# Retention and two MLPs on one core: padded queries, narrower states, and another order in the opening

## The chip, the cores and the metric

The kernel runs on one core of a Trainium2 chip. The metric is the device time of one execution in microseconds. Three runs of the kernel before gave 868.02, 868.12 and 868.51 us; the median is 868.12 us.

## What is computed

Four batches, 8 heads, 576 positions, head width 64. A retention (attention without softmax, with a decay by distance) is followed by two MLPs of width 512 to 2048 to 512 on 2304 tokens.

```python
scores = (1 / np.sqrt(64)) * np.matmul(q, k.transpose(0, 1, 3, 2))
gamma = 1.0 - 2.0 ** (-5.0 - np.arange(H))
ret = scores * np.where(rel >= 0, gamma[:, None, None] ** rel, 0.0)   # rel = row position - column position
x = np.matmul(ret, v).transpose(0, 2, 1, 3).reshape(2304, 512)
h = x @ moe_w_in;   x = softplus(h) @ moe_w_out
h = x @ moe2_w_in;  out = (h * sigmoid(1.702 * h)) @ moe2_w_out
```

## The kernel before

Heads are taken in pairs, two heads stacked on the 128 partitions (`halves`, L278). The positions of a batch go in chunks of 128: pair (b, p) has a first step c = 0 with chunks 0 and 1 and a second step c = 1 with chunks 2 and 3 and the last 64 positions. One batch has 8 such steps; the text numbers them 0 to 7, step i being pair i//2, c = i%2. The program is written out in full and each engine works through its own instructions in the order of the text.

One step of the retention is `step` (L301). It forms for each chunk a state update (`sums`, L336: decayed keys times values, in PSUM), the scores of the chunk (L345, into `ps`), and, for the step `out_i` handed in beside it, the output products: states times queries (L323) and masked scores times values (L326, L328). Behind them come: the states taken from PSUM (`svs`, one tile of 128x128 for two heads, whose two 64x64 blocks on the diagonal are filled one by one, L354 to L361; the rest was set to zero once at L470), the scores scaled into `a` (ACT at L366 in the first batch) and masked by GpSimd's affine_select (L370), the tail's scores (L378), and the output times its decay into `xf` (L384) and `xt` (L389).

The first batch is `first_batch` (L415): loads of all 8 steps of keys, queries and values (`kqv`, 512 KB each), the batch's last positions (`ends`, 640 KB at once), decays, and the raw words of the first weights (`w1_load`, two transfers of 512 KB each for one f), all on the SP queue. Then ten rounds follow: round i does `scale_pair(i + 1, True)` (L297, both halves of the keys times their decay, on GpSimd), `step(i - 2, i)`, in odd rounds from 3 on `split_x` (the result is split into a high part on ACT, `xh`, and a low part on DVE, `xl`, which waits in `late` for the next round), and one warming product (`warm`, L458). `warm` is also called WARM = 14 times at the start, on a tile that nothing else uses.

The weights of the first MLP arrive as 64-bit words and are converted by `convert` (L100), a generator of five pieces per weight f: ACT L109, then DVE L121 and L122, then DVE L126, then ACT L92 (the high half), then DVE L97 (the low half, which is followed by L109 of the next f). The loop at L502 advances it once per round from index 4 on, the index being the round plus one. After the rounds `pre` (L1039) loads f + 4 and advances it until f + 2 weights are made; `side` (L512) advances it and the retention of the next batch (`batch`, L396, one third of a step at a time) between the products of the first MLP. That MLP is `run_first` (L149): `mm1(f)`, 12 products with `w1_in[f]`, softplus, and two turns later `mm2(f)`, 12 products with `w1_out[f]`; all of them are recorded on L147. The tiles of the weights, the raw words and the loads of the first batch share one pool, `wp`, with 16 places.

Of the kernel before, what the change touches and what calls it, by code (L numbers as in the profile page):

```python
# [15 lines left out]
P = 128  # L16
# [5 lines left out]
WARM = 14  # L22
# [10 lines left out]
def kernel(  # L33
# [190 lines left out]
    with tc.manual_schedule():  # L224
# [37 lines left out]
        with ExitStack() as consts, ExitStack() as right, ExitStack() as second:  # L262
# [4 lines left out]
            mask = ac.tile([P, 5, D], F32, name="mask")  # L267
# [4 lines left out]
            svs = [[ac.tile([P, P], F32, name=f"sv{i}_{j}") for j in range(4)] for i in range(2)]  # L272
# [8 lines left out]
            def load_pair(i, tile_of=None, end_of=None):  # L281
# [7 lines left out]
                v = t[:, 2 * C0:].rearrange("p (t s d) -> p t s d", t=2, s=2)  # L289
                loaded[i] = t[:, 0:C0], t[:, C0:2 * C0], v[:, :, 0, :], v[:, :, 1, :], e  # L290

            def scale_pair(i, pool=False):
                p, x = pairs[i][2], loaded[i][2]
                for h in range(2):
                    y, d = x[:, :, halves[h]], sdec[:, 2 * p + h:2 * p + h + 1]
                    if pool:
                        nc.gpsimd.tensor_scalar(out=y, in0=y, scalar1=d, scalar2=None, op0=ALU.mult)  # L297
                    else:
                        nc.scalar.mul(y, y, d)

            def step(out_i, i, banks, on_act, later, early=False):  # L301
# [12 lines left out]
                if out_i is not None:  # L314
# [4 lines left out]
                    for t in range(2 + c):  # L319
                        j = slice(t * P, t * P + (P if t < 2 else D))  # L320
                        if states[t] is not None:
                            for h, r in enumerate(halves):
                                put(h, j, states[t][:, r], q[:, j] if t < 2 else e[:, P:P + D])  # L323
                        for h, r in enumerate(halves):
                            if t < 2:
                                put(h, j, v[:, t, r], a[:, h * C0 + t * P:h * C0 + (t + 1) * P])  # L326
                            else:
                                put(h, j, e[:, P + D + h * D:P + D + (h + 1) * D], a[:, 2 * C0:])  # L328
                if i is not None:
                    b, c, p = pairs[i]  # L330
                    k, q, x, v, e = loaded[i]
                    if c:
                        for h, r in enumerate(halves):
                            put(h, ends_at, e[:, r], e[:, P:P + D])
# [15 lines left out]
                if i is not None:  # L350
                    b, c, p = pairs[i]
                    states = [None] + svs[p % 2] if c == 0 else svs[p % 2][1:]
                    for t in range(2):
                        for r in halves:  # L354
                            sv, new = states[t + 1][r, r], po[r, cols[t]]
                            if states[t] is None:
                                hi("a" if len(on_act) == 2 else "v", sv, new)
                            else:
                                nc.vector.scalar_tensor_tensor(  # L359
                                    out=sv, in0=states[t][r, r], scalar=gdec[r, p:p + 1], in1=new,  # L360
                                    op0=ALU.mult, op1=ALU.add)  # L361
                    a = ap.tile([P, 2 * C0 + D], F32, tag="a", name="a", bufs=2)
                    for h in range(2):
                        ah, rd = a[:, h * C0:(h + 1) * C0], rdec[:, 2 * p + h:2 * p + h + 1]
                        if h in on_act:
# [9 lines left out]
                            out=ah, in0=ps[h][:, 0:C0], scalar=rd,  # L375
                            in1=mask[:, 0:4, :].rearrange("p t j -> p (t j)"), op0=ALU.mult, op1=ALU.mult)
                    if c:
                        nc.vector.scalar_tensor_tensor(  # L378
                            out=a[:, 2 * C0:], in0=po[:, ends_at], scalar=r2dec[:, p:p + 1],
                            in1=mask[:, 4, :], op0=ALU.mult, op1=ALU.mult)  # L380
# [34 lines left out]
            def first_batch():  # L415
# [3 lines left out]
                raw = [wp.tile([P, 2, KQV], F32, tag="w", name="w_kqv") for _ in range(NPAIR)]  # L419
                end = wp.tile([P, 2, KQV], F32, tag="w", name="w_end")  # L420
                end = end.rearrange("p s n -> p (s n)")[:, 0:NPAIR * ENDS].rearrange("p (a n) -> p a n", a=NPAIR)

                def load(i):
                    load_pair(i, raw[i // 2][:, i % 2], end[:, i // 2])
# [15 lines left out]
                for i in range(n + 2):  # L440
# [31 lines left out]
            nc.gpsimd.affine_select(  # L472
                out=mask[:, 0:4, :].rearrange("p (t u) j -> p t (u j)", u=2),
                in_=mask[:, 0:4, :].rearrange("p (t u) j -> p t (u j)", u=2), compare_op=ALU.is_ge, fill=0.0,
# [685 lines left out]
```

## Time and profile before

| | us |
|---|---|
| median of three runs | 868.12 |
| the profiled execution | 867.95 |
| its span, first to last instruction | 866.2 |
| PE busy in the span | 847.8 |
| DVE, ACT, POOL busy | 582.3, 405.6, 100.9 |

The span is cut into stretches in the first group of rows below; a stretch shows how long each engine was busy in it. PE is TensorE's products, PEld its weight loads, DVE VectorE, ACT ScalarE, POOL GpSimd, SP the queue that issues transfers. A product with 512 columns is counted busy for longer than the distance to the next one, because products overlap.

### The profile page before, as it was taken

The page shows a single profiled execution, that of the slowest core. Times are in us where ns is not written, and L with a number is a line of the kernel's source. Part 1 is how long each engine was busy: PE and PEld are TensorE (multiplying, and loading weights), DVE is VectorE, ACT ScalarE, POOL GpSimd, SP SyncE. Part 2 cuts the span into 40 slices and gives each one's busy share as a digit, 9 for nine tenths or more (in the row PEclk, how much of TensorE's full clock was granted, in tenths as well). Part 3 has the DMA queues.
Part 4 walks back from the last instruction along what each step waited for, and adds up shares of the span by engine and source line. Part 5 has one row for each costly group of instructions (what it writes and reads, how often), then busy time and mean ns, then how long its engine had stood idle before and what let it go on. Part 6 is the DMA issues. An engine that isn't in the chain of part 4 may idle for free.

```text
span 866.2 us, 15721 instructions
## 1 busy us (share of the span) xinstructions
PE 847.8 (98%) x6163; PEld 760.4 (88%) x6167; DVE 582.3 (67%) x1173; ACT 405.6 (47%) x803; POOL 100.9 (12%) x183
## 2 busy tenths in 40 slices
PE   8799999999999999999999999999999999999997
PEld 5478888887878888899888899999999999999997
DVE  4998983767667766577443467788778777866521
ACT  4556554334454443456333555555555555554321
POOL 5200000100111011101101121201021112011100
PEclk9999999999999999999999999999999999999999
DMA  9925532787979766599996597888797779776621
GB/s 357 395 85 202 183 119 86 231 251 272 289 232 300 264 222 216 206 366 344 370 372 218 184 344 246 308 304 293 244 330 279 268 248 331 265 275 222 217 73 24
DMA packets 62633, 217.30 MB, mean 251 GB/s; under 512 B 6368, under 2 KB 20704, under 8 KB 50272
## 3 DMA queue, kind: packets, MB, share of 16 engines
q1 hardware_dynamic: 44992, 111.96, 37.2%
q0 software_dynamic: 17568, 104.34, 33.7%
q8 instruction: 48, 0.79, 0.4%
q14 instruction: 25, 0.20, 0.1%
HBM read 157.56 MB, written 58.72 MB: 250 GB/s over the span
## 4 chain that ended last, share of the span: by engine, by line
PE 54%; issue 31%; DVE 7%; POOL 3%; DMA 2%; ACT 1%; POOLq 0%; DVEq 0%; ACTq 0%
PE ph L711 15%; PE m L711 14%; PE ph L147 10%; PE y L147 9%; PE y L711 3%; PE ps_h L311 2%; DVE wa L122 1%; DMA xo<-x 1%; DVE wa L126 1%; POOL w L630 1%; POOL whole_out L548 1%; PE ps_s L345 1%; POOL whole_in L548 1%; PE ps_warm L465 1%; DVE sv L359 1%
## 5 line engine op out<-in xcount | busy, mean ns | idle before, releaser
L147 PE MATMUL y<-gh,w 128*128 128x512 f32 (+1 forms) x640 | 196.9, 371 | 0.8 <-DVE yb L94 0.8
L147 PE MATMUL ph<-xh,w 128*128 128x512 f32 (+1 forms) x640 | 184.6, 372 | 5.8 <-DVE w L97 1.5
L147 PEld LDWEIGHTS ph<-xh,w 128*128 128x128 f32 x640 | 114.5, 189 | 29.4 <-DVE w L97 2.1
L147 PEld LDWEIGHTS y<-gh,w 128*128 128x128 f32 x640 | 117.2, 188 | 22.0 <-DVE yb L94 1.0
L147 PE MATMUL ph<-xl,w 128*128 128x512 f32 (+1 forms) x320 | 118.1, 369 | 0.5 <-DVE xl L97 0.5
L147 PE MATMUL y<-gl,w 128*128 128x512 f32 (+1 forms) x320 | 117.8, 368 | 0.0
L711 PE MATMUL m<-w,ga 128*128 128x256 f32 x768 | 117.2, 282 | 0.6 <-DVE yb L783 0.6
L711 PE MATMUL ph<-xo_c,w 128*128 128x256 f32 x768 | 108.3, 283 | 0.0
L97 DVE TENSOR_TENSOR gl<-g,gh 128x512 fp32r<-128x512 f32 (+1 forms) x80 | 50.9, 636 | 83.6 <-ACT gh L92 82.8
L711 PE MATMUL ph<-xo,w 128*128 128x256 f32 x768 | 105.9, 283 | 0.8 <-DVE ho L977 0.5
L711 PEld LDWEIGHTS m<-w,ga 128*128 128x128 f32 x768 | 102.8, 190 | 1.1 <-PE ph L711 1.1
L711 PEld LDWEIGHTS ph<-xo,w 128*128 128x128 f32 x768 | 97.6, 189 | 2.3 <-DVE ho L977 1.6
L711 PEld LDWEIGHTS ph<-xo_c,w 128*128 128x128 f32 x768 | 97.9, 188 | 1.4 <-DVE he L939 0.6
L194 ACT ACTIVATE g<-ph 128x512 f32<-128x512 f32 (+1 forms) x80 | 44.1, 552 | 107.6 <-PE ph L147 104.5
L711 PE MATMUL m<-w,gb 128*128 128x256 f32 x576 | 89.7, 282 | 0.0
L711 PEld LDWEIGHTS m<-w,gb 128*128 128x128 f32 x576 | 78.0, 191 | 0.0
L147 PEld LDWEIGHTS ph<-xl,w 128*128 128x128 f32 x320 | 60.3, 189 | 11.0 <-DVE xl L97 0.9
L147 PEld LDWEIGHTS y<-gl,w 128*128 128x128 f32 x320 | 60.4, 189 | 9.3
L92 ACT CAST halves<-wa 128x512 fp32r<-128x512 f32 x32 | 19.8, 620 | 84.1 <-DMA kept<-halves 33.4
L97 DVE TENSOR_TENSOR ga<-g,ga 128x512 fp32r<-128x512 f32 x72 | 47.1, 686 | 9.2 <-ACT ga L92 9.2
L92 ACT CAST ga<-g 128x512 fp32r<-128x512 f32 x72 | 44.8, 622 | 15.4 <-PE y L711 7.9
L97 DVE TENSOR_TENSOR halves<-wa,halves 128x512 fp32r<-128x512 f32 x32 | 22.1, 692 | 39.6 <-ACT halves L92 39.1
(151 smaller groups left out, 1182.4 us busy)
## 6 DMA issues: line engine op xcount, KB each, us to landing
w<-sums_in POOLq DMA_DIRECT2D x32, 1024.0 KB, 5.8
w<-sums_out POOLq DMA_DIRECT2D x32, 1024.0 KB, 7.6
raw<-kqv SPq DMA_DIRECT2D x24, 512.0 KB, 4.7
w<-kept POOLq DMA_DIRECT2D x12, 1024.0 KB, 8.2
w_raw<-w_in SPq DMA_DIRECT2D x16, 512.0 KB, 9.1
w_raw<-w_out SPq DMA_DIRECT2D x16, 512.0 KB, 9.5
raw<-w_in SPq DMA_DIRECT2D x16, 512.0 KB, 4.2
raw<-w_out SPq DMA_DIRECT2D x16, 512.0 KB, 4.4
```

The source lines that it names most:

```text
L92: nc.scalar.copy(dst, src)
L97: nc.vector.tensor_tensor(out=dst, in0=src, in1=f32(h), op=ALU.subtract)
L122: nc.vector.scalar_tensor_tensor(out=u, in0=u, scalar=3, in1=high, op0=ALU.logical_shift_left, op1=ALU.bitwise_or)
L126: nc.vector.scalar_tensor_tensor(out=u, in0=low, scalar=29, in1=u, op0=ALU.logical_shift_right, op1=ALU.bitwise_or)
L147: nc.tensor.matmul(out_ap, l, r, start=first and i == 0, stop=last and i == k - 1)
L194: nc.scalar.activation(g, ph, AF.Softplus)
L311: nc.tensor.matmul(po[halves[h], at], l, rhs, start=clear[h], stop=True, skip_group_check=True)
L345: nc.tensor.matmul(ps[h][:, j], k[r, j], q[r, j], start=True, stop=True)
L359: nc.vector.scalar_tensor_tensor(out=sv, in0=states[t][r, r], scalar=gdec[r, p:p + 1], in1=new, op0=ALU.mult, op1=ALU.add)
L465: nc.tensor.matmul(warm_at["y"], x[:, 0:P], x, start=True, stop=True)
L548: nc.gpsimd.dma_start(out=whole_d[j, s][:, o, :], in_=a)
L711: nc.tensor.matmul(out_ap, l, r, start=clear, stop=True, skip_group_check=True)
```

## The change

Queries come zero-padded per head (64 rows of the head, 64 rows of zeros), so each step's load holds keys, two padded query blocks, and keys and values by position: 640 KB in place of 512. With padded queries a state needs no zeros beside it, so it is one tile of 128x64 for both heads, written by one instruction where there were two, and the tiles need no clearing. The same holds for the last 64 positions: the queries are padded and the keys are not. The mask is stored once (128x128) and read with a broadcast. WARM goes from 14 to 8. In the first batch, one of the two key scalings goes from GpSimd to ACT, each step has its own tile, the ends are four transfers of 160 KB behind the odd steps' loads, the first weight is loaded behind step 2 in place of step 3, and the second to fourth weights are loaded at the end of the first batch's program text. The conversion starts one round earlier, pauses at index 8, and the last `xl` comes ahead of the conversion's next piece.

```diff
-WARM = 14
+WARM = 8
-            mask = ac.tile([P, 5, D], F32, name="mask")
+            mask = ac.tile([P, 1, P], F32, name="mask")
+            mask_t = ac.tile([P, D], F32, name="mask_t")
-            svs = [[ac.tile([P, P], F32, name=f"sv{i}_{j}") for j in range(4)] for i in range(2)]
+            svs = [[ac.tile([P, D], F32, name=f"sv{i}_{j}") for j in range(4)] for i in range(2)]
...
-                    if pool:
+                    if pool and h:
                         nc.gpsimd.tensor_scalar(out=y, in0=y, scalar1=d, scalar2=None, op0=ALU.mult)
                     else:
                         nc.scalar.mul(y, y, d)
...
-                                put(h, j, states[t][:, r], q[:, j] if t < 2 else e[:, P:P + D])
+                                put(h, j, states[t], q[:, h, j] if t < 2 else e[:, D + h * D:2 * D + h * D])
...
-                            nc.tensor.matmul(ps[h][:, j], k[r, j], q[r, j], start=True, stop=True)
+                            nc.tensor.matmul(ps[h][:, j], k[r, j], q[r, h, j], start=True, stop=True)
...
-                        for r in halves:
-                            sv, new = states[t + 1][r, r], po[r, cols[t]]
-                            if states[t] is None:
-                                hi("a" if len(on_act) == 2 else "v", sv, new)
-                            else:
-                                nc.vector.scalar_tensor_tensor(
-                                    out=sv, in0=states[t][r, r], scalar=gdec[r, p:p + 1], in1=new,
-                                    op0=ALU.mult, op1=ALU.add)
+                        sv, new = states[t + 1], po[:, cols[t]]
+                        if states[t] is None:
+                            hi("a" if len(on_act) == 2 else "v", sv, new)
+                        else:
+                            nc.vector.scalar_tensor_tensor(
+                                out=sv, in0=states[t], scalar=gdec[:, p:p + 1], in1=new,
+                                op0=ALU.mult, op1=ALU.add)
...
                 def load(i):
-                    load_pair(i, raw[i // 2][:, i % 2], end[:, i // 2])
+                    t = wp.tile([P, 4 * DM], F32, tag="w", name="w_kqv")
+                    e = t[:, KQV:KQV + ENDS]
+                    load_pair(i, t[:, 0:KQV], e)
+                    if i % 2:
+                        nc.sync.dma_start(out=e, in_=ends[0, :, i // 2])
                 load(0)
                 nc.sync.dma_start(out=dec, in_=decays)
                 load(1)
-                nc.sync.dma_start(out=end, in_=ends[0])
                 nc.sync.dma_start(out=odec, in_=outdecay)
-                for i in range(2, 4):
+                load(2)
+                w1_load(0)
+                for i in range(3, n):
                     load(i)
-                w1_load(0)
-                for i in range(4, n):
-                    load(i)
-                w1_load(1)
...
+                    if i == n + 1:
+                        late.pop()()
                     for _ in range(FILL if i < n + 1 else 0):
                         warm()
                     yield
-                while late:
-                    late.pop()()
...
-            for sv in svs[0] + svs[1]:
-                nc.vector.memset(sv, 0.0)
...
             for i, _ in enumerate(first_batch()):
-                if i in (4, 7):
-                    w1_load(i // 3 + 1)
-                if i >= 4:
+                if i in (8, 9, 10):
+                    w1_load(i - 7)
+                if i >= 3 and i != 8:
                     next(w1_gen, None)
```

## Rows read from the trace of the kernel before

**Rows 1.** Stretches: us, busy per engine (instructions), PEclk, DMA share, GB/s

```profile
15.00:30.00 15.00, 12.89 (x191) 10.41 (x194) 13.42 (x34) 9.47 (x20) 10.65 (x13) 1.00 1.03 408
30.00:45.00 15.00, 10.10 (x42) 6.44 (x36) 13.80 (x18) 7.87 (x12) 0.00 (x0) 1.00 0.88 349
45.00:60.00 15.00, 15.00 (x101) 12.24 (x101) 13.71 (x19) 10.12 (x15) 0.63 (x2) 1.00 0.23 79
...
100.00:400.00 300.00, 297.82 (x1971) 250.00 (x1970) 202.90 (x422) 133.91 (x256) 25.33 (x47) 1.00 0.69 234
```

**Rows 2.** Timeline, first products of the MLP: start, length, engine, line [idle before]

```profile
30.06 0.73 PE L147 MATMUL ph<-xh,w 128*128 128x512 f32 x2
...
35.55 1.23 DVE L97 TENSOR_TENSOR w<-wa,w 128x1024 fp32r<-128x1024 f32 x1 [0.51 <-ACT w L92]
...
36.83 0.50 PE L147 MATMUL ph<-xh,w 128*128 128x512 f32 x1 [0.76 <-DVE w L97]
```

**Rows 3.** Timeline, conversion of the third weight on DVE and ACT

```profile
36.69 0.69 DVE L121 TENSOR_SCALAR w_raw<-w_raw 128x1024 uint32<-128x1024 uint32 x1
...
37.42 1.23 DVE L122 SCALAR_TENSOR_TENSOR wa<-wa,w_raw 128x1024 uint32<-128x1024 uint32 x1
...
38.67 1.23 DVE L126 SCALAR_TENSOR_TENSOR wa<-w_raw,wa 128x1024 uint32<-128x1024 uint32 x1
...
39.94 1.04 ACT L92 CAST w<-wa 128x1024 fp32r<-128x1024 f32 x1 [2.24 <-DVE wa L126]
40.89 1.15 ACT L109 ACTIVATE wa<-w_raw 128x1024 f32<-128x1024 f32 x1
```

**Rows 4.** DVE groups by shape, 0 to 30 us: count, busy us and mean ns, idle

```profile
L359 DVE SCALAR_TENSOR_TENSOR sv<-sv,dec,ps_y 64x64 f32<-64x64 f32 x16 | 4.5, 279 | 1.5 <-PE ps_y L311 1.1
L359 DVE SCALAR_TENSOR_TENSOR sv<-sv,dec,ps_h 64x64 f32<-64x64 f32 x8 | 2.2, 280 | 7.5 <-ACT sv L92 7.4
L97 DVE TENSOR_TENSOR xl<-xf,xh 128x512 fp32r<-128x512 f32 x3 | 2.2, 736 | 0.6 <-ACT xh L92 0.6
...
L384 DVE TENSOR_TENSOR xf<-ps_h,odec 128x256 f32<-128x256 f32 x3 | 1.3, 425 | 0.1
...
L378 DVE SCALAR_TENSOR_TENSOR a<-ps_y,dec,mask 128x64 f32<-128x64 f32 x4 | 1.1, 284 | 0.1
```

**Rows 5.** POOL groups by shape, 0 to 30 us

```profile
L297 POOL TENSOR_SCALAR w_kqv<-w_kqv,dec 128x128 f32<-128x128 f32 x16 | 11.9, 752 | 2.5 <-DMA dec<-decays 1.5 <-DMA w_kqv<-kqv 1.0
L370 POOL TENSOR_SCALAR_AFFINE_SELECT a<-a 128x512 f32<-128x512 f32 x8 | 5.6, 698 | 5.8 <-ACT a L366 4.2 <-issue 1.6
```

**Rows 6.** ACT groups by shape, 0 to 45 us

```profile
L366 ACT ACTIVATE a<-ps_y,dec 128x256 f32<-128x256 f32 x8 | 3.4, 471 | 3.6 <-PE ps_y L345 1.9 <-POOL a L370 1.7
L92 ACT CAST xh<-xf 128x512 fp32r<-128x512 f32 x4 | 2.5, 618 | 6.0 <-DVE xf L384 6.0
...
L92 ACT COPY sv<-ps_h 64x64 f32<-64x64 f32 x8 | 1.6, 204 | 8.1 <-PE ps_h L311 8.0
...
L299 ACT ACTIVATE raw<-raw,dec 128x128 f32<-128x128 f32 x2 | 0.7, 404 | 0.0
```

**Rows 7.** Waits of the SP queue, 0 to 80 us: total, times, longest

```profile
SPq L488 <- DMA w_kqv<-kqv: 5.7, 6, 1.1
```

**Rows 8.** Timeline of SP: issues of weights that waited for kqv loads

```profile
11.80 0.33 SPq L488 DMA_DIRECT2D w_raw<-w_out  x1
...
19.85 0.33 SPq L488 DMA_DIRECT2D w_raw<-w_out  x1
```

**Rows 9.** Timeline of PE: warming products, then one round of the retention

```profile
1.51 6.12 PE L465 MATMUL ps_warm<-warm 128*128 128x512 bf16 x14 [1.51 <-DVE warm L462]
...
13.27 0.44 PE L311 MATMUL ps_y<-w_kqv,sv 128*64 128x128 f32 x4
...
14.87 0.71 PE L345 MATMUL ps_y<-w_kqv 64*128 64x128 f32 x8
```

**Rows 10.** Durations of the warming products, 0 to 40 us: min/median/max ns

```profile
L465 PE MATMUL ps_warm<-warm x19: 389/634/634, 1.5 to 28.3; 128*128 128x512 bf16 x19
```

More of the change, by code (lines that the diff above doesn't have):

```diff
@@ L288, in load_pair @@
                     nc.sync.dma_start(out=e, in_=ends[b, :, p])
-                v = t[:, 2 * C0:].rearrange("p (t s d) -> p t s d", t=2, s=2)
-                loaded[i] = t[:, 0:C0], t[:, C0:2 * C0], v[:, :, 0, :], v[:, :, 1, :], e
+                q = t[:, C0:3 * C0].rearrange("p (h n) -> p h n", h=2)
+                v = t[:, 3 * C0:].rearrange("p (t s d) -> p t s d", t=2, s=2)
+                loaded[i] = t[:, 0:C0], q, v[:, :, 0, :], v[:, :, 1, :], e
             def scale_pair(i, pool=False):
@@ L333, in step @@
                         for h, r in enumerate(halves):
-                            put(h, ends_at, e[:, r], e[:, P:P + D])
+                            put(h, ends_at, e[:, 0:D], e[:, D + h * D:2 * D + h * D])
                     def sums():
@@ L374, in step @@
                         nc.vector.scalar_tensor_tensor(
-                            out=ah, in0=ps[h][:, 0:C0], scalar=rd,
-                            in1=mask[:, 0:4, :].rearrange("p t j -> p (t j)"), op0=ALU.mult, op1=ALU.mult)
+                            out=ah.rearrange("p (t j) -> p t j", t=2),
+                            in0=ps[h][:, 0:C0].rearrange("p (t j) -> p t j", t=2), scalar=rd,
+                            in1=mask.to_broadcast([P, 2, P]), op0=ALU.mult, op1=ALU.mult)
                     if c:
@@ L379, in step @@
                             out=a[:, 2 * C0:], in0=po[:, ends_at], scalar=r2dec[:, p:p + 1],
-                            in1=mask[:, 4, :], op0=ALU.mult, op1=ALU.mult)
+                            in1=mask_t, op0=ALU.mult, op1=ALU.mult)
                     masked[i] = a
@@ L468 @@
                 warm()
-            for sv in svs[0] + svs[1]:
-                nc.vector.memset(sv, 0.0)
             nc.vector.memset(mask, 1.0)
             nc.gpsimd.affine_select(
-                out=mask[:, 0:4, :].rearrange("p (t u) j -> p t (u j)", u=2),
-                in_=mask[:, 0:4, :].rearrange("p (t u) j -> p t (u j)", u=2), compare_op=ALU.is_ge, fill=0.0,
-                base=0, pattern=[[0, 2], [1, P]], channel_multiplier=-1)
-            for h, r in enumerate(halves):
-                nc.vector.tensor_copy(mask[r, 4, :], mask[r, h, :])
+                out=mask, in_=mask, compare_op=ALU.is_ge, fill=0.0,
+                base=0, pattern=[[0, 1], [1, P]], channel_multiplier=-1)
+            for r in halves:
+                nc.vector.tensor_copy(mask_t[r], mask[r, 0, r])
             raws = {}
@@ L1127 @@
     kq = np.stack([k, q], 2).transpose(0, 1, 4, 2, 3).reshape(B, H // 2, P, 2, S)
-    by_d = kq[..., 0:T2].reshape(B, H // 2, P, 2, 2, C0).transpose(0, 4, 1, 2, 3, 5).reshape(B, 2, H // 2, P, T2)
+    by_d = np.zeros((B, 2, H // 2, P, 3, C0), np.float32)
+    by_h = kq[..., 0:T2].reshape(B, H // 2, 2, D, 2, 2, C0).transpose(0, 5, 1, 2, 3, 4, 6)
+    for h in range(2):
+        r = slice(h * D, (h + 1) * D)
+        by_d[:, :, :, r, 0] = by_h[:, :, :, h, :, 0]
+        by_d[:, :, :, r, 1 + h] = by_h[:, :, :, h, :, 1]
+    by_d = by_d.reshape(B, 2, H // 2, P, 3 * C0)
     kv = np.stack([k, v], 2)[:, :, :, 0:T2].reshape(B, H // 2, 2, 2, 2, 2, P, D)
@@ L1133 @@
         r = slice(h * D, (h + 1) * D)
-        last[:, :, r, h * D:(h + 1) * D] = kq[:, :, r, 0, T2:]
-        last[:, :, r, P + D + h * D:P + D + (h + 1) * D] = v[:, h::2, T2:]
-    last[..., P:P + D] = kq[..., 1, T2:]
+        last[:, :, r, D + h * D:2 * D + h * D] = kq[:, :, r, 1, T2:]
+        last[:, :, r, 3 * D + h * D:4 * D + h * D] = v[:, h::2, T2:]
+    last[..., 0:D] = kq[..., 0, T2:]
     last = last.transpose(0, 2, 1, 3)
-    d, o = _decays(H)
     d, o = _decays(H)
```

5 lines of the change are left out of this document (1 added, 4 removed).

## The prediction, made before the changed kernel ran

> **What bounds the kernel now.** Read the stretches first [rows 1]. From 45 us on PE is busy without a break, and from 100 to 400 us it stands still for 2.2 us of 300; what DVE and ACT save there is beside work that PE does anyway. Between 15 and 45 us PE stands still for 7.0 of 30 us, and DVE is busy for 27.2 of the same 30. This change can win only there. Then read the timeline where the first MLP begins [rows 2]: its first product starts at 30.06 us, but the second weight decides what follows. Its low half is written by DVE from 35.55 to 36.78 us, and the product that waits for it starts at 36.83. The third weight follows by a fixed chain of DVE and ACT pieces [rows 3], and when it is there, at 42 us, PE has enough to do to the end. So one number decides: the moment W when the second weight's low half is written, 36.78 us now. Each microsecond that W comes earlier, all of the rest comes earlier, and an earlier first product alone wins nothing: PE then waits longer for W.
>
> **State updates.** Two instructions of 64x64 become one of 128x64. One of 64x64 takes 0.28 us on DVE [rows 4], and a DVE instruction of 128x64 takes the same 0.284 us [rows 4], since only partitions are added. In the first batch an even step saves one copy on ACT, 0.2 us [rows 6], and one DVE instruction; an odd step saves two DVE instructions. That is 4 x 0.28 + 4 x 0.56 = 3.4 us of DVE in the first batch, 2.2 us of it in steps 3 to 7. The later batches save as much beside a busy PE: counted as 0.2 us, from bounds of 0 and the 2.2 us that PE stands still there [rows 1]. The products keep their shapes: 64 columns of weights and 128 moving columns, with zeros now in the queries. PE time is unchanged. The mask, its broadcast and the clearing that is left out (before the first data) cost nothing on the path; if the broadcast slowed the masked scores of the later batches, these lie beside PE's work as well.
>
> **Loads.** A load grows from 512 to 640 KB. Six weight issues waited on the SP queue for a kqv load to land [rows 7]; counted along the queue it is each time the transfer eight before, which dates the landings: the weight transfer at 11.80 us waited for load 3, that at 19.85 us for load 7 [rows 8]. From 15 to 30 us the engines carry 408 GB/s [rows 1]. Up to and with load 3, 4 x 512 + 12 + 640 + 256 = 2956 KB were ahead; now it is 4 x 640 + 12 + 160 + 256 + 1024 = 4012 KB, as the first weight moves ahead of it. 1056 KB more at 408 GB/s are 2.6 us: load 3 lands at 14.4 in place of 11.8 us. Load 7 has 6892 KB in place of 6028 with it, 2.2 us: 22.0 us. The second weight lands 2048 KB (by the old count at load 7) behind that mark, 5.1 us, at 25 us; by the sum below it is wanted at 29 us. That cover is 4 us; gone, W would go with it. The four smaller transfers of the ends are 3 issues more on the SP queue at 0.33 us each [rows 8], in a queue that waits for landings anyway, so nothing.
>
> **Key scaling.** On GpSimd one scaling takes 0.75 us on average beside DVE's work and a mask 0.70 [rows 5]; on ACT one takes 0.35 [rows 6]. GpSimd loses 8 scalings, ACT gets 8 of 0.35 us, 2.8 us. What is new: the scaling of step i + 1 stands in ACT's queue ahead of the state copy and the scores of step i, and waits for load i + 1. So the scores of step i, on which mask, output and decay follow, now wait for the next load, and the scaling in turn waits behind the high-part copies on ACT.
>
> **Start.** WARM = 8 ends at 1.51 + 8 x 0.43 = 4.95 us, where 14 end at 7.63 [rows 9]. The first load is 128 KB longer, 0.3 us. GpSimd's first scaling waited for the decays behind that load, 1.5 us of idle time [rows 5], so data and not PE is what the start then waits for. Steps 0 to 2 get 1 to 2 us earlier, and lose it again at load 3.
>
> **The sum to W.** I add each engine's queue in the order of the text, from load 3 at 14.4 us. ACT: scaling 3 (0.35 [rows 6]), state copy (0.2), two scores (0.83), rebase of the first weight L109 (1.15 [rows 3]), scaling 4, scores of step 3, first high part (0.62 [rows 6]), scaling 5, copy, scores of step 4: 20.4 us without a gap. From there the round closes over PE: an odd round takes 1.6 us from its first output product to its scores and the scores 0.7 [rows 9]. Output of step 3 starts at 19.85 (its mask waited beside DVE's L121 and L122), sums 5 end at 21.6, scores at 22.2; scores on ACT 23.1, high part 23.8, high half of the first weight (1.04 [rows 3]) 24.85, scaling 7 25.2, sums 7 26.2, their scores 26.9, ACT 27.8, mask 28.5, output of step 7 from 28.75 to 30.15. DVE meanwhile: low part 30.1, two outputs (0.42 [rows 4]) 30.9, then ACT's last high part 31.55 and DVE's low part 32.3, which now stands ahead of the conversion. Second weight: L121 33.0, L122 34.25, L126 35.5, high half 36.6, low half W = 37.9. The same additions made on the kernel before end at W = 38.1 where the trace has 36.78: a group's first instruction releases its reader before the group ends, and I count whole groups. So the sum is 1.3 too late there, and likewise here: W = 36.6, 0.2 us earlier. From below, W is bounded by DVE alone: from 15.1 us it has 18.5 us of work up to W, and 1.1 us of waiting for the high half that nothing fills: 34.7. From above stands the uncorrected sum, 37.9. What DVE saved (2.2 us) is paid back by the late load 3, by ACT's longer queue, and by the low part ahead of the conversion. The first product starts near 29.5 and the first twelve end near 32, 3.5 us earlier than now, and PE waits for W.
>
> 867.95 - 0.2 - 0.2 (later batches) = 867.55 for a profiled execution; the median of the runs lay 0.17 above it: **867.7 us**. With W from 34.7 to 37.9: 865.8 to 869.1.
>
> **Rivals.** First, faster: DVE fills the gaps in which it waits, because in the trace of before it is busy for 27.2 of 30 us and the overlap may be as tight after. Then W nears its bound of 34.7, and the time 865.8 to 866.3. For it: the same additions were 1.3 us too late before. Against: load 3 at 14.4 holds everything behind it, and ACT is full from there to 20.4.
>
> Second, slower: PE falls to its lower clock. The trace shows the granted clock as 1.00 in all these stretches [rows 1], but the products themselves show the level: the warming product takes 634 ns in the opening burst and 389 later [rows 10], and 14 of them take 6.12 us, 0.43 us for 512 columns, which is the 1.2 GHz level; full speed came only after all 14 [rows 9]. The change leaves 8 and a wait for data behind them, and it opens a gap of about 4 us between the first twelve products and W in which PE has one product. Before, PE is busy for 10.1 of 15 us there [rows 1] and its products stay fast. If the clock falls in that gap, it decides when PE has to run dense, from W on: PE needs as much work as in the first burst, 6.1 us at half rate, to get it back, and loses half, 3.1 us: 870.8. If it stays low in the opening up to 20 us instead, each round of 2.3 us takes twice that for rounds 3 and 4, of which load waits hide about 1.5: also near +3 us.
>
> The Trainium skill, "TensorE: Matmul & The Clock Gate", section "What's actually happening", says that the slow clock is the default and that only activity releases it; section "HAM oscillation — how this bites in real kernels" has matmul bursts between data waits going cold again each time. By that rule this change, which opens a data wait ahead of the dense part, would end at the time of the second rival; the trace agrees on the start (634 ns first, 389 later), and no gap of this length stands in the stretch before it.
>
> Third, the transfers of later batches: 24 loads of 128 KB more, 0.3 us each at 408 GB/s. Exposed in one of ten they cost 1 us; the stretch of 100 to 400 us uses 0.69 of the DMA engines [rows 1], so I take none.
>
> **How the numbers follow.** A difference under 0.2% (1.7 us: below 866.4 or above 869.9) is about what a measurement of this kernel can tell from no change. The forecast has 0.55; the first rival 0.23, most of it under 866.4; the clock 0.19 and transfers with something else 0.03. Between the ends, 865.7 to 870.8 leaves out about 2 in 10 or less.
>
> **What would show it.** Right: the low half of the second weight ends at 36 to 37.5 us, and the first product starts at 29 to 30 with a wait of 3 to 5 us behind the first twelve. Load 3 lands near 14.4: GpSimd's or ACT's scaling of step 3 starts there. State instructions take 0.28 us at 128x64, half as many. Wrong: W under 35 (DVE without gaps), products of 0.63 us behind 30 us (the clock), scalings that start well before 14 us (loads faster than counted), or PE gaps in the later batches that differ by over 1 us.

## The result, and the profile after

The changed kernel takes 877.05 us (median of 7 runs, 872.40 to 878.51) against 868.12 us for the kernel before (7 runs, 866.67 to 870.09). The ratio is 1.0092, with an interval from 1.0070 to 1.0115: it is slower by about 9 us, where 867.7 was forecast and 870.8 was the upper end. The profiled execution took 877.53 us with a span of 875.5 us, 9.3 us more than the 866.2 of before.

The first question is where these 9.3 us lie. The first view is that of the stretches of the changed kernel, with the columns of [rows 1]:

```profile
15.00:30.00 15.00, 13.95 (x206) 11.06 (x203) 12.73 (x31) 10.75 (x24) 9.49 (x10) 1.00 1.02 406
30.00:45.00 15.00, 10.40 (x35) 6.96 (x33) 12.61 (x14) 7.59 (x11) 0.00 (x0) 0.89 1.03 410
100.00:400.00 300.00, 292.12 (x1893) 242.50 (x1892) 182.71 (x364) 127.45 (x243) 24.95 (x46) 0.99 0.68 230
```

In the opening PE does no worse than before; the third weight is complete at 42.30 us in place of 42.24. But from 100 to 400 us PE stands still for 7.9 us where it stood still for 2.2 [rows 1]. DVE and ACT are busy for *less* time there than before (182.7 and 127.5 us against 202.9 and 133.9), and still somebody waits for them. (For DVE this is less work, 563.2 against 582.3 us over the whole span. ACT has as much as before, 406.4 against 405.6 us; it only comes to it later.) PE's waits from 147 to 425 us say for whom. The view gives the line that waited, what it waited for, then total, times and longest. First the kernel before, then the changed one:

```profile
PE y L147 <- DVE yb L94: 0.8, 1, 0.8
PE ph L147 <- ACT g L194: 0.7, 1, 0.7
PE ph L147 <- DVE xf L384: 0.6, 1, 0.6
```

```profile
PE ph L147 <- ACT g L194: 2.7, 2, 1.9
PE ph L147 <- ACT xh L92: 2.5, 1, 2.5
PE y L147 <- DVE yb L94: 1.5, 1, 1.5
PE ph L147 <- DVE xf L386: 0.7, 2, 0.4
PE ph L147 <- DVE xl L97: 0.6, 1, 0.6
```

The longest wait for `xh` stands at the end of batch 1, near 247 us. The long wait for `g`, 1.9 us, ends at 319.84 us and stands in the middle of batch 2, which ends only at 356 us. ACT's timeline around both (start, length, then in brackets the idle time before and what ended it):

```profile
234.05 0.62 ACT L92 CAST halves<-wa 128x512 fp32r<-128x512 f32 x1 [2.16 <-DMA kept<-halves]
...
240.47 0.62 ACT L92 CAST halves<-wa 128x512 fp32r<-128x512 f32 x1 [4.09 <-DMA kept<-halves]
240.99 0.67 ACT L109 ACTIVATE wa<-raw 128x512 f32<-128x512 f32 x1
245.20 0.62 ACT L92 CAST halves<-wa 128x512 fp32r<-128x512 f32 x1 [3.54 <-DMA rest_out<-halves]
245.73 0.59 ACT L194 ACTIVATE g<-ph 128x512 f32<-128x512 f32 x1
...
247.44 2.16 ACT L92 CAST xh<-xf 128x512 fp32r<-128x512 f32 x4
...
318.68 0.62 ACT L92 CAST halves<-wa 128x512 fp32r<-128x512 f32 x1 [7.28 <-DMA kept<-halves]
319.20 0.59 ACT L194 ACTIVATE g<-ph 128x512 f32<-128x512 f32 x1
```

`halves` is the converted second-MLP weight. It is written into a staging tile and stored to DRAM (`kept`, `rest_out`, `rest_in`), and the tag of these tiles, `raw64`, has three buffers, two of which hold raw words read ahead. So the next weight's high half, on ACT, waits until the store of the weight before has landed. Behind it in ACT's queue stand the softplus `g` and the copies `xh` of the next batch's activations; they start without a wait of their own, so their inputs were there. PE meets the first of the two waits as follows:

```profile
245.26 0.39 PE L147 MATMUL y<-gh,w 128*128 128x512 f32 x1
248.10 0.73 PE L147 MATMUL ph<-xh,w 128*128 128x512 f32 x2 [2.45 <-ACT xh L92]
249.41 0.78 PE L147 MATMUL ph<-xl,w 128*128 128x512 f32 x1 [0.58 <-DVE xl L97]
249.99 1.05 PE L147 MATMUL ph<-xh,w 128*128 128x512 f32 x2
250.85 0.63 PE L147 MATMUL ph<-xl,w 128*128 128x512 f32 x1
...
253.63 0.39 PE L147 MATMUL ph<-xl,w 128*128 128x512 f32 x1
```

Two things are to be seen: an idle stretch of 2.45 us, a pair of products and 0.58 us more; and behind it products of 0.63 us, which take 0.39 from 253.6 us on. The granted clock shows the same behind both waits (stretch, its length, PE's busy time and products, granted clock, DMA share, GB/s):

```profile
249.00:253.00 4.00, 3.59 (x20) 0.57 0.43 155
320.00:324.00 4.00, 4.00 (x12) 0.64 0.39 131
```

So the 9.3 us are two sums. PE's idle time over the span grows from 18.4 us (866.2 - 847.8) to 23.9 (875.5 - 851.6), 5.5 us, and PE's busy time grows from 847.8 to 851.6 us, 3.8 us. Both lie behind the opening: from 45 us on, for 5821 products in either trace, the idle time grows from 9.0 to 14.8 us and the busy time from 812.2 to 815.7 us, as some products run at the 1.2 GHz level behind a stall.

ACT's waits from 147 to 325 us, before and after, name the cause that the experiments then have to test:

```profile
ACT halves L92 <- DMA kept<-halves: 29.9, 10, 5.4
ACT g L194 <- PE ph L147: 28.7, 14, 4.6
ACT halves L92 <- DMA rest_out<-halves: 12.6, 3, 5.1
```

```profile
ACT halves L92 <- DMA kept<-halves: 45.1, 10, 7.3
ACT g L194 <- PE ph L147: 18.4, 9, 5.5
ACT halves L92 <- DMA rest_out<-halves: 13.3, 3, 5.8
```

ACT waited for these stores for 42.5 us before as well, and PE felt nothing of it. After it is 58.4 us, and PE does. The row for `g` shows how far ACT is ahead of PE: where ACT waits for PE's `ph`, it is early. It does so for 28.7 us before and for 18.4 after. The stores themselves land no later in the changed kernel: for the 512 KB ones of `kept` from 150 to 325 us the median from issue to landing is 3.8 us, where it was 4.0.

### The profile page after: what moved, and what is told of

The parts are those of the page before. It is cut to its first block, busy times and chain, and to the rows that moved or that the text cites. A ratio compares the mean times of both kernels' runs of the same rounds, so it can differ in the third digit from the quotient of the medians.

```text
span 875.5 us, 15651 instructions
## 1 busy us (share of the span) xinstructions
PE 851.6 (97%) x6161; PEld 763.0 (87%) x6161; DVE 563.2 (64%) x1105; ACT 406.4 (46%) x807; POOL 97.6 (11%) x175
## 4 chain that ended last, share of the span: by engine, by line
PE 70%; issue 17%; DVE 5%; DMA 3%; POOL 2%; ACT 1%; SPq 0%; POOLq 0%; DVEq 0%; ACTq 0%
PE ph L708 19%; PE m L708 16%; PE ph L147 14%; PE y L147 14%; PE y L708 3%; PE ps_h L313 2%; DMA x<-x_lo 1%; PE ps_s L347 1%; DMA w_kqv<-kqv 1%; POOL whole_out L545 1%; POOL whole_in L545 1%; DMA rest_out<-halves 1%; PE ps_y L313 1%; DMA y<-yb 0%; DVE wa L126 0%
## 5 line engine op out<-in xcount | busy, mean ns | idle before, releaser
L147 PE MATMUL ph<-xh,w 128*128 128x512 f32 (+1 forms) x640 | 187.0, 376 | 10.4 <-ACT w L92 3.1
L147 PE MATMUL ph<-xl,w 128*128 128x512 f32 (+1 forms) x320 | 120.0, 375 | 0.6 <-DVE xl L97 0.6
```

Of the source, the lines that this page charges most:

```text
L147: nc.tensor.matmul(out_ap, l, r, start=first and i == 0, stop=last and i == k - 1)
```

## The experiments

Each run stands beside runs of the kernel before on the same chip, and the ratio is to those (their medians lie between 867.92 and 869.23 us). The table has all of them. W is the end of the second weight's low half, as in the prediction; "rest" is the span less W, all that comes behind the opening; the next column is ACT's total wait for the stores of `halves` from 147 to 325 us, the last PE's waits from 147 to 425 us. The median and the ratio are of all runs; the other columns are of the one profiled execution, which can lie off the median (e3 2.4 us under it, e14 2.0 us over it). The expectations give ACT's wait as 33 us for the kernel before and 47 for the changed one: these are the waits for `kept` alone, over the whole span.

| kernel | median us | ratio, 95% interval | span | W | rest | ACT for stores | PE waits |
|---|---|---|---|---|---|---|---|
| before | 868.12 | 1 | 866.2 | 36.8 | 829.4 | 42.5 | 2.1 |
| after | 877.05 | 1.0070 to 1.0115 | 875.5 | 36.8 | 838.7 | 58.4 | 8.0 |
| e1 before + dead bytes | 871.37 | 1.0027 to 1.0053 | 870.6 | 36.5 | 834.1 | 53.5 | 5.6 |
| e2 after, no zeros moved | 870.24 | 1.0009 to 1.0037 | 868.3 | 37.6 | 830.7 | 52.1 | 2.8 |
| e3 after, old opening | 873.15 | 1.0043 to 1.0086 | 869.0 | 36.0 | 833.0 | 56.9 | 4.6 |
| e4 before, new opening | 872.40 | 1.0026 to 1.0062 | 870.5 | 37.5 | 833.0 | 48.2 | 5.2 |
| e5 after, hold | 879.78 | 1.0116 to 1.0154 | 878.4 | 37.6 | 840.8 | 60.9 | 9.4 |
| e6 before, hold | 875.73 | 1.0077 to 1.0112 | 872.5 | 36.8 | 835.7 | 52.8 | 7.7 |
| e7 before, two steps later | 879.33 | 1.0086 to 1.0153 | 879.0 | 36.6 | 842.4 | 57.1 | 5.6 |
| e8 after, two steps later | 881.08 | 1.0124 to 1.0163 | 878.6 | 37.6 | 841.0 | 60.9 | 10.7 |
| e9 after + buffer | 869.17 | 0.9993 to 1.0020 | 865.8 | 36.3 | 829.5 | 2.3 | 2.8 |
| e10 before + buffer | 868.41 | 0.9983 to 1.0010 | 867.0 | 37.0 | 830.0 | 0 | 2.1 |
| e11 after + buffer, later | 868.20 | 0.9980 to 0.9999 | 866.0 | 36.3 | 829.7 | 21.1 | 2.7 |
| e12 before + buffer, later | 866.98 | 0.9965 to 0.9984 | 865.0 | 36.7 | 828.3 | 20.0 | 1.0 |
| e13 e11, old opening | 865.80 | 0.9956 to 0.9977 | 863.8 | 35.9 | 827.9 | 25.9 | 0.7 |
| e14 e12, new opening | 870.39 | 1.0000 to 1.0025 | 870.6 | 40.2 | 830.4 | 20.8 | 2.4 |
| e15 e11, no zeros moved | 865.67 | 0.9948 to 0.9975 | 864.4 | 37.4 | 827.0 | 26.6 | 0.7 |
| e16 e13, no zeros moved | 865.32 | 0.9939 to 0.9968 | 863.7 | 36.1 | 827.6 | 28.1 | 0.7 |

**Bytes, opening or states (e1 to e4).** The first four ask which part of the change is to blame. e1 adds to the kernel before only bytes: behind each later load 128 KB are copied from DRAM to DRAM, which nothing reads.

```
                 nc.sync.dma_start(out=t, in_=kqv[b, c, p])
+                if tile_of is None:
+                    nc.sync.dma_start(out=dead_d[i % 4], in_=kqv[b, c, p][:, 0:C0])
```

> The kernel before, with 128 KB more moved behind each later load of keys, queries and values (from DRAM to DRAM, read by nobody, one transfer more per load). Nothing else differs. Theory T1 (bytes: the larger loads delay the stores of the second MLP's converted weights, ACT waits for a store's buffer, PE stands still at the ends of the batches and its clock falls): 872 to 878 us, ACT's wait for the stores (33 us in the kernel before, 47 in the changed one) over 42 us. Theory T2 (the opening's new order shifts everything behind it into a worse meeting) and theory T3 (fewer state instructions let the conversion run into the stores earlier): 868 us, within 1.5.

Measured 871.37 us, between the two ranges, with 53.5 us of waits for the stores. e2 is the changed kernel whose later loads leave the zeros out; they are set once in three fixed tiles, and each load goes in three transfers.

```
-                nc.sync.dma_start(out=t, in_=kqv[b, c, p])
+                t, src = kept_raw[i % RB], kqv[b, c, p]
+                nc.sync.dma_start(out=t[halves[0], 0:2 * C0], in_=src[halves[0], 0:2 * C0])
...
+                nc.sync.dma_start(out=t[:, 3 * C0:], in_=src[:, 3 * C0:])
```

> The changed kernel, with the zeros of the queries written once into three fixed tiles, so a later load moves 512 KB again (in three transfers in place of one). T1: 866 to 869 us, PE's idle time from 100 to 400 us back to 2 to 3 us, no fall of the granted clock there. T2 and T3: 874 to 878 us. If three transfers in place of one cost something by themselves, it comes out above T1's time.

Measured 870.24 us, above T1's range and below the others'. e3 and e4 exchange the openings (WARM, who scales, the order of the first loads and conversions): e3 is the changed kernel with the opening of before, e4 the kernel before with the changed opening, both just as the diff has them.

> The changed kernel with the opening of the kernel before: 14 warming products, both key scalings on GpSimd, first weight behind step 3, second weight behind step 7, conversion from index 4, low part late; padding, states and per-step tiles stay. T1 and T3: 873 to 878 us, with the same stalls from 220 to 320 us. T2: 867 to 869 us.

> The kernel before with the changed kernel's opening alone: 8 warming products, one key scaling on ACT, ends in four transfers, the order of weights, conversion and low part; no padding, 512 KB loads, old states. T2: 874 to 878 us. T1 and T3: 867 to 868.5 us, as the second weight would be ready no later than 36.8 us (load 3 lands 1.1 us earlier than in the changed kernel).

Measured 873.15 and 872.40 us. So bytes alone cost 3 us, the opening alone 4, padding with its bytes and states 5, all together 9, and with the bytes taken out 2 remain. No theory of one part gives that: each edit that shifts something loses some us, and all of them behind the opening. The opening's own mark W moves by at most 0.8 us, in both directions, while "rest" grows from 829.4 to 831 and up to 839.

**Where the batch ends (e5, e6).** The next theory took the stall at its face: ACT is held by a conversion copy just when a batch ends, so no conversion step should be issued there. A batch passes through the 16 weights f one after another; the hold covers the last of these sixteenths in batches 1 and 2, and the rate of the conversion is raised in the others.

```
-W2RATE = 1.1
+W2RATE = 1.18
...
+                if 1 <= i < B - 1:
+                    conv["rate"] = W2RATE if f < NF - 1 else 0.0
```

> The changed kernel with one edit: in the last sixteenth of batches 1 and 2 no step of the second weights' conversion is issued (its rate goes from 1.1 to 1.18 in the other fifteen, so as many steps in all). Theory: the loss is made where a batch ends, because ACT's queue holds a conversion copy that waits for a store to land, and the copies of the next batch's activations (xh, g) stand behind it; PE then waits 2 to 2.5 us twice and its clock falls. By it the PE stalls near 246 and 319 us are gone, the y_t store starts at 408 to 410 us and the median is 868 to 871. Rival A (the 128 KB more per load slow PE's surroundings everywhere, the place of the conversion doesn't matter): 875 to 878. Rival B (the opening's loss is carried along): 873 to 876.

> The same hold of the conversion in the kernel before. Theory: there nothing waits at the batch ends that a hold could save (PE stands still for 2.2 us in 300), so 867 to 869. If the hold helps by something other than the batch ends (the rate of 1.18 alone), it gains here too, 865 or less. If the raised rate costs, 870 or more.

Measured 879.78 us for e5, 2.7 us more than the changed kernel, and 875.73 for e6, 7.8 more than before: the theory in this form is wrong. The longest of PE's waits of e5:

```profile
PE ph L147 <- DVE xf L386: 6.0, 2, 3.2
```

The wait for `xh` is gone as meant, but PE now waits for `xf`: the retention's product bank in PSUM is shared with the MLP's `ph`, and DVE, which empties it, comes late in its turn. ACT waits for stores for 60.9 us, no less than in the changed kernel. Two things keep e5 and e6 from saying more. The hold could not reach the wait at 319.84 us, which is not at the end of a batch. And the two long waits of e5 lie ahead of the hold, in the sixteenths with the raised rate of 1.18:

```profile
222.21 1.19 PE L147 MATMUL ph<-xh,w 128*128 128x512 f32 x2 [2.85 <-DVE xf L386]
...
314.02 1.16 PE L147 MATMUL ph<-xh,w 128*128 128x512 f32 x2 [3.16 <-DVE xf L386]
```

The expectation of e6 had named this ("if the raised rate costs, 870 or more"), and 875.73 us fits it. The hold and the rate were not run apart, so what the hold alone does is not shown.

**The phase alone (e7, e8).** These two change no byte, no instruction and nothing of the opening: the second weights' conversion only begins two steps later.

```
                 w2_read(1)
-                for _ in range(8):
+                for _ in range(10):
```

> The kernel before, and only the second weights' conversion begins two steps later (10 empty steps in place of 8, about 2 us or half of one weight's round). No byte, no instruction and nothing of the opening is changed. Theory: the loss hangs on where the round stands when the batch ends, so this alone moves the time, by 2 to 5 us to 870 to 873, with PE waits for ACT's xh or g near 245 or 319 us. Rival (only more bytes or a changed opening do it): 868 +- 0.8.

> The changed kernel, and only the second weights' conversion begins two steps later. Theory: the place of the round at the batch end decides, so the time moves from 877 by 2 us or more, and by the size of the earlier losses downwards, 869 to 875; the stalls near 245 and 319 us change place or size. Rival (bytes): 876 to 878.5.

Measured 879.33 us for e7: this alone costs the kernel *before* 11 us, more than the whole change. e8 went up too, to 881.08, where a fall was expected; the sign was wrong, only the sensitivity was right. PE's longest waits of e7 are again for `g` and `xh`:

```profile
PE ph L147 <- ACT g L194: 3.0, 2, 2.7
PE ph L147 <- ACT xh L92: 1.9, 1, 1.9
```

and ACT's timeline shows the copies `xh`, and then `g`, behind a store:

```profile
245.52 0.62 ACT L92 CAST halves<-wa 128x512 fp32r<-128x512 f32 x1 [3.49 <-DMA rest_out<-halves]
246.04 2.17 ACT L92 CAST xh<-xf 128x512 fp32r<-128x512 f32 x4
...
254.22 0.62 ACT L92 CAST halves<-wa 128x512 fp32r<-128x512 f32 x1 [4.83 <-DMA kept<-halves]
254.75 0.59 ACT L194 ACTIVATE g<-ph 128x512 f32<-128x512 f32 x1
```

The wait for `xh` is at the same place as in the changed kernel, the end of batch 1; the long one for `g` follows 9 us later, where the changed kernel has its own at 319.84 us. Of the 12.8 us of span that e7 has over the kernel before, 8.6 are slower products (busy 856.4 against 847.8 us) and 4.2 idle time: its granted clock is 0.79 from 244 to 268 us, and 0.99 even behind 600 us.

So the kernel before comes through batches 1 and 2 well by the place at which its conversion happens to stand, and each edit tried so far loses that.

**The wait itself taken away (e9 to e12).** One more buffer for the staging tiles lets the next weight's high half be written while the store of the last one is under way. The room comes from the rebased words `wa`, which need 2 KB each for the second weights and were given 4; the first weights' `wa` take the shared tag (the last two lines are the two callers of the conversion).

```
-    t = wr.tile([P, DM, 2], U32, tag="raw64", name="raw64", bufs=3)
+    t = wr.tile([P, DM, 2], U32, tag="raw64", name="raw64", bufs=4)
...
-    w2_half["t"] = wr.tile([P, 2, DM], F32R, tag="raw64", name="halves", bufs=3)
+    w2_half["t"] = wr.tile([P, 2, DM], F32R, tag="raw64", name="halves", bufs=4)
...
-    a = wr.tile([P, 2 * DM], F32, tag="wa", name="wa")[:, 0:w.shape[1]]
+    a = a_tile(i, w.shape[1])
...
+    lambda i, k: wr.tile([P, 2 * DM], F32, tag="raw64", name="wa", bufs=4))
...
+    lambda i, k: wr.tile([P, k], F32, tag="wa", name="wa"))
```

e9 and e10 are the two kernels with this buffer; e11 and e12 have the buffer and the begin of e7 and e8.

> The changed kernel with one more buffer for the second weights' raw words and converted halves (four tiles of 4 KB in place of three; the room comes from the rebased words, which need 2 KB each here). Theory: one weight's round is held by the store of the weight before (halves has one free buffer, so ACT's high half waits 2 to 6 us for that store), ACT's queue runs late, and PE waits for what stands behind. With the buffer those waits (47 us of ACT between 150 and 320 us) fall under 10 us, the PE waits for ACT near 245 and 319 us go, and the median is 866 to 869. Rival A (contention of the bytes themselves): waits move to the raw reads, 874 to 878. Rival B (only half of the loss): 870 to 873.

> The same buffer in the kernel before. Theory: ACT's 33 us of waits for stores fall under 10 us; PE had 2.2 us of idle time there to gain, so 866 to 868.5. If the time rises to 870 or more, the place of the round counts by something other than these stores.

> The changed kernel with the buffer, and the conversion begun two steps later. Theory: with the buffer the phase no longer counts: within 1.5 us of the run with the buffer alone. Rival (phase counts by itself): 4 us or more apart, as the shift alone moved the kernel before by 11 us.

> The kernel before with the buffer, and the conversion begun two steps later. Theory: within 1.5 us of the run of before with the buffer alone, where without the buffer the same shift cost 11 us. Rival: 874 to 880 as without the buffer.

Measured 869.17, 868.41, 868.20 and 866.98 us, as the theory said, but for e9, which is 0.2 us above its range. The changed kernel gets 7.9 us back by the medians (7.5 by the ratios, 1.0092 and 1.0006). The kernel before gets nothing, since PE had nothing to get there. And the shift by two steps, which cost the kernel before 11 us without the buffer and the changed one 4, now saves 1.4 and 1.0. ACT's longest waits of e9 from 147 to 325 us:

```profile
ACT g L194 <- PE ph L147: 58.4, 21, 5.5
ACT halves L92 <- DVE wa L126: 35.0, 15, 5.3
ACT halves L92 <- DMA kept<-halves: 2.3, 2, 1.4
```

58.4 us of waits for stores have become 2.3, and ACT is now early: it waits 58.4 us for PE (by chance the same figure), where it was 18.4 in the changed kernel. At the end of batch 1 of e9 no store holds it:

```profile
238.45 0.60 ACT L194 ACTIVATE g<-ph 128x512 f32<-128x512 f32 x1 [0.47 <-PE ph L147]
...
240.19 2.17 ACT L92 CAST xh<-xf 128x512 fp32r<-128x512 f32 x4
```

This settles the cause: bytes, opening and states of e9 are those of the changed kernel, and its edit touches buffers alone. The part of that edit which reaches the first weights (their `wa` has four shared places where it had two) does not carry the gain: W moves from 36.8 to 36.3 us, and from 45 to 147 us PE is busy throughout in both.

The total of ACT's waits for stores is not by itself what sets the time. With the late begin it is 20 to 28 us again (e11 to e16), and PE's waits stay at 0.7 to 2.7 us; the kernel before had 42.5 and lost nothing. What sets the kernels with the buffer apart is that ACT is early: from 147 to 325 us it waits for PE's `ph` for 47.9 to 61.3 us in e9 to e16, and for 15.1 to 34.5 us in the ten kernels without it. Then a wait for a store ends before PE needs what stands behind it. Among those ten, this number does not order the times (34.5 us in e7); there the place of the single waits decides.

**What the change costs without that wait (e13 to e16).** e13 and e14 are e3 and e4, e15 is e2, each with the buffer and the late begin; e16 is e15 with the opening of before.

> The changed kernel with the buffer and the late begin, and with the opening of before (14 warming products, both halves scaled on GpSimd, first weight behind load 3): padding and states alone, without the wait for stores. Without the buffer this pair cost 4.8 us against before (873.15). Theory: nothing is left of it, 866.5 to 868. Rival (the bytes cost by themselves): 869.5 or more. If the opening holds the 1.2 us that the changed kernel keeps with the buffer, this run equals before with the buffer, 867.

> The kernel before with the buffer and the late begin, and with the opening of the changed kernel alone. Without the buffer the opening cost 4.1 us (872.4). Theory: 867 to 868.5, since its PE waits in the opening (3.5 us for the second weight's high half, 3.1 for the third's) stand in place of the earlier waits. Rival (the opening itself loses): 870 or more.

> The changed kernel with the buffer and the late begin, its later loads moving 512 KB without the zeros. Theory (bytes count only through the store wait): within 1 us of 868.2, the run with the zeros moved. Rival (bytes keep a price of their own): 867 or less.

> The three edits that each helped together: the changed kernel's states and padded queries, the buffer with the late begin, the opening of before, and later loads without the zeros (512 KB). If the gains of the old opening (2.4 us against the changed opening, both with the buffer) and of the zeros left out (2.5 us) add, 863.3; if they meet in the same waits, 865 to 866, as each alone. Over 868 would mean that the three transfers per load disturb the old opening's round.

Measured 865.80, 870.39, 865.67 and 865.32 us. These ran on other chips than e11 and e12, so the ratios are compared. Padding and states alone (e13) cost nothing any more: 0.9967 against 0.9975 for e12, with intervals that overlap; W is 35.9 in place of 36.7. The 4.8 us that they cost in e3 went with the buffer and the late begin. The changed opening alone (e14, 1.0012) loses 0.37% or 3.2 us against e12, beyond the 867 to 868.5 expected; its rival, that the opening itself loses, is what came. In the profiled executions (that of e14 is the slowest of its twelve) 3.5 of the 5.6 us between e12 and e14 lie ahead of the dense part; this is the second weight's low half in e12 and in e14:

```profile
35.51 1.22 DVE L97 TENSOR_TENSOR w<-wa,w 128x1024 fp32r<-128x1024 f32 x1 [0.51 <-ACT w L92]
```

```profile
38.98 1.23 DVE L97 TENSOR_TENSOR w<-wa,w 128x1024 fp32r<-128x1024 f32 x1 [1.11 <-ACT w L92]
```

In e14 ACT's scaling of the third load starts at 10.31 us, in e4, with the same opening, at 8.19, each when the load has landed; why it landed 2.1 us later is open. Against e11 (0.9990), going back to the old opening (e13) saves 0.23% or 2.0 us and leaving the zeros out (e15, 0.9962) 0.28% or 2.4 us, but both together (e16, 0.9954) only 0.36%: the two gains hardly add, and what they share was not taken apart further. So the theory of e15, that bytes count only through the wait for stores, is wrong: its interval (0.9948 to 0.9975) lies clear of that of e11 (0.9980 to 0.9999), as its rival had it. The gain lies behind the opening (rest 827.0 against 829.7 us, with W 1.1 us later); where it comes from is not shown.

e13, e15 and e16 are faster than both kernels; e16 by 0.46% (0.32 to 0.61%) against before. e13 is the plainer one: padding and states of the change, the opening of before, the fourth buffer and the late begin.

## Why the prediction was wrong, point by point

**W and the opening: right, the closeness in part by luck.** The whole working went into W, and W held: 36.6 us was forecast, and the low half ends at 35.61 + 1.22 = 36.83. Load 3, forecast to land at 14.4, releases ACT's scaling at 14.23; the first MLP product starts at 29.46 (29 to 30 forecast); PE then waits for the second weight's high half, about as long as said:

```profile
14.23 0.40 ACT L301 ACTIVATE w_kqv<-w_kqv,dec 128x128 f32<-128x128 f32 x1 [3.01 <-DMA w_kqv<-kqv]
...
35.61 1.22 DVE L97 TENSOR_TENSOR w<-wa,w 128x1024 fp32r<-128x1024 f32 x1 [1.11 <-ACT w L92]
35.63 0.50 PE L147 MATMUL ph<-xh,w 128*128 128x512 f32 x1 [3.14 <-ACT w L92]
```

The warming products end at 1.51 + 3.59 = 5.10 us (4.95 forecast), and a state update of 128x64 takes 0.28 us, half as many. Taken apart, the opening alone makes W later (37.5 in e4, 40.2 in e14), padding and states alone make it earlier (36.0 in e3, 35.9 in e13), and together they cancel, as the sum had it ("paid back by the late load 3, by ACT's longer queue"). That the hit is within 0.2 us is in part luck: e5 and e8, which differ from the changed kernel only from batch 1 on, have W at 37.6. A slip in the working did no harm: its ACT terms from 14.4 us add to 20.1, not 20.4, and the trace has 19.65.

**The first rival**, DVE without gaps and W near 34.7, did not happen: W is where the sum had it. No run has a W under 35.9.

**The clock rival: right in what happens, wrong in its place.** In the opening the clock falls, in the gap before W: from 35 to 42 us the granted clock is 0.76, and products take 0.63 us from 37.99 on. It is not the change that brings this: e6 and e7 have the opening of before untouched, and their granted clock there is 0.52 and 0.76, where the one trace that the prediction had read shows 1.00. And it cost nothing there, as the third weight is complete only at 42.30 us (42.24 before) and the slow products wait for it anyway; the price of 3.1 us assumed that PE had work, and 6.1 us at the low clock, where products are back at 0.40 us by 42.69. It did cost in batches 1 and 2: from 45 us on PE is busy for 3.5 us more, for as many products.

The Trainium skill, "TensorE: Matmul & The Clock Gate", section "HAM oscillation — how this bites in real kernels", describes bursts that go cold between waits for data. The trace agrees in that the clock falls behind waits at three places of the changed kernel (a granted clock of 0.76, 0.57 and 0.64); these waits were for ACT, and the last two came out of long dense stretches. Before, the waits in the two later stretches were 0.8 us and less, and the granted clock is 1.00 there.

**The step that failed** is the cover of the later batches. The prediction wrote that "from 100 to 400 us it stands still for 2.2 us of 300; what DVE and ACT save there is beside work that PE does anyway", costed the later batches at a gain of 0.2 us, and gave the 128 KB more per load a price of 1 us at most, with a chance of 0.03 together with whatever else there might be, because the DMA engines are used to 0.69 there. Each of these numbers is read rightly. The conclusion from them was not: that PE stands still for only 2.2 us was taken for slack, and it was a meeting that could fail. The row that says so is in the trace of before: ACT's waits, 29.9 and 12.6 us for stores in 178 us. An engine that is busy for 45% of the time and waits in order for a store, ahead of work that PE needs, is not cover. What the runs showed in its place is 5.8 us more of idle time and 3.5 us of slower products behind 45 us, and 7.9 us back with one more buffer.

How little room a round had can be put together from the rows. A weight's round goes from one high half (0.62 us) through the low half (0.69), the issue of the store (0.52) and its landing to the next high half. The store issued at 235.43 us let ACT go on at 240.47, 5.0 us later, so that round took 6.4 us (234.05 to 240.47). The mean round of e9, where almost nothing waits for a store, is 6.1 us (32 high halves from 152.21 to 341.26 us). So a store that takes 5.0 us holds its round beyond the mean, and the delay goes to what stands behind it on ACT; with the median landing of 3.8 us the same round would take some 5.2, an estimate. Why the changed kernel waits 16 us more for stores that land no later is not shown; its larger loads do land later (median from 150 to 325 us: 4.9 us before, 6.2 after), and so do the reads of raw words (4.2 and 4.4 before, 4.5 and 4.8 after).

The Trainium skill, "DMA: Bandwidth & Descriptors", section "Anatomy of one DMA — SWDGE (gpsimd) path", puts a fixed part of about 2.0 us, most of it the receipt of the write, beside the bytes at 436 GB/s, for transfers that GpSimd issues. For 512 KB that would be an estimate of 3.2 us. The median here is 3.8 us, on the SP queue and beside other transfers. By either number the store is most of a round of 6.1 us.

**What the prediction had named as a sign of its being wrong** was the right one: "PE gaps in the later batches that differ by over 1 us". They differ by 5.9 (8.0 against 2.1 us).

## What to carry to other kernels

That the busiest engine hardly stands still says that the kernel meets its dates, not that there is slack behind them: before costing a change "beside other work" at nothing, read the waits of the engines that hand over to it, in order, and ask what stands behind each long one. A staging tile that is stored to DRAM and has one free buffer makes the engine that fills it wait for landings (42.5 to 60.9 us of 178 here); whether that costs anything depends on what stands behind it, and a second buffer takes the question away. And where two steps' shift of a background task moves the time by more than the change does, take that coupling away first and measure the change after.

## What the runs showed of the hardware

In the changed kernel, an idle time of 2.45 us, one pair of products and 0.58 us more at the end of batch 1, and a single wait of 1.91 us in batch 2, each came ahead of a fall of PE's granted clock to the 1.2 GHz level for some 4 us; products then take 0.63 in place of 0.39 us. It is not certain to fall: e8 has the longest single wait of all there, 3.4 us, and its granted clock from 240 to 330 us is 1.00. In the opening of before, untouched, the granted clock from 35 to 42 us is 1.00 in one execution and 0.52 and 0.76 in others (e6, e7). What makes the difference is open. In the kernels with the buffer the longest wait of PE from 147 to 425 us is 2.0 us, and the granted clock from 147 to 420 us is 1.00 in all of them. In e9 5.2 us of PE waits less (8.0 - 2.8) go with 9.7 us less of span.
